# Sorting the values of other items as a row pair, with the first tail laid out by hand

## The chip, the cores and the metric

The kernel runs on one core of a Trainium2 chip. The metric is device time in microseconds (us), measured over whole executions. A trace of one execution gives the span from the first to the last instruction; it is about 2 us shorter than the measured time. The kernel before has a median of 172.65 us. Times in the trace are counted from the start of the span.

## The reference

For each of four items (batch elements) and eight heads, the reference makes a doubly normalised 8 x 8 matrix P from `sort_net`, mixes the eight blocks of 96 keys and of 96 values with it ("sorts" them), attends within each block, and passes the result through a layer with a maximum of two products.

```python
for _ in range(5):                       # P: 4 x 8 x 8 x 8
    P = exp(P - max(P)); P = P / sum(P, -1); P = P / sum(P, -2)
k_sorted = einsum('bhij,bhjcd->bhicd', P, k_blocks)
v_sorted = einsum('bhij,bhjcd->bhicd', P, v_blocks)
attn = softmax(scale * q_blocks @ k_sorted.T)     # within each block
x = (attn @ v_sorted) laid out as 3072 tokens x 512
out = maximum(x @ w1, x @ w2) @ w_out
```

In the text, items are counted from one (item two is `b == 1` in the code).

## The kernel before

TensorE (PE) does nearly everything; VectorE (DVE) and ScalarE (ACT) copy TensorE's results out of its accumulation memory PSUM ("evict" it), exponentiate and normalise; GpSimd (POOL) issues the loads that convert to bf16; SyncE (SP) issues outputs and DMA transposes. The work of one item's feed-forward part is cut into units, and the attention of the next item is strewn between them. What comes after a unit is listed in `tail`, or spread evenly as `steps`.

An item's values fill 64 partitions: two items lie side by side in the 128 rows of `v_raw`. VectorE turns them into `v_dc`, from which TensorE takes its weights. Items one and two are sorted singly (`sort_v`, one row half); items three and four as a pair (`sort_v_pair`, matmuls alternating between the halves).

```python
def load_v(b, c0=0, pieces=2):
    r0 = (b % 2) * 64
    ...
        nc.gpsimd.dma_start(out=v_raw[r0 : r0 + 64, ...], in_=v_src[b, :, ...])

def sort_v(b, t, n=0, eng=None):           # 16 matmuls of one row half, one eviction
    r0, m0 = (b % 2) * 64, (b % 2) * 64
    for m in range(16):
        nc.tensor.matmul(ps[:, m * 64 : (m + 1) * 64],
            v_weights(slice(r0, r0 + 64), t * 16 + m), bd_v[b][r0 : r0 + 64, :], ...)
    evac(...)

def sort_v_pair(b, t, eng=None):           # 8 matmuls of each half in turn, one eviction
    for m in range(8):
        for par in range(2):
            rows = slice(par * 64, par * 64 + 64)
            nc.tensor.matmul(ps[:, par * 512 + m * 64 : ...], v_weights(rows, t * 8 + m),
                bd_v[b][rows, :], ...)
    evac(...)

def x_transposes(b, t, eng=None):          # activations into the layout of the products
    if b:                                  # items two to four: by DMA, issued on SP
        nc.sync.dma_start_transpose(out=xT[:, b % 2, ih, hh]..., in_=x...)
        return
    ...                                    # item one: on TensorE

tail = {
    2: [VA[6], TR[2], VA[7]],
    3: [TR[3], lambda: w2_transposes(1, "A")(), load_rest],       # load_q(1), load_k(2)
    4: [lambda: turn(second, 0)],  ...
    9: [lambda: load_v(2), lambda: load_v(3), lambda: load_k(3)],
    14: [lambda: load_q(2)],
    18: [lambda: pair_q(2, 0), lambda: pair_q(2, 1), lambda: load_q(3)],
}
```

`q_raw` has one buffer, so `load_q(3)` (item four's queries) starts when `pair_q(2)` has read item three's. `xT` is what the products `h` of the next item read; TensorE cannot start them before the transposes have landed.

The softmax here doesn't subtract the row's maximum and nothing guards it: scores larger than these inputs give would overflow.

## Time and profile before

| | before |
|---|---|
| median time | 172.65 us |
| span of the profiled run | 170.8 us |
| TensorE busy | 162.3 us, 95% |
| VectorE, ScalarE busy | 44%, 50% |
| granted TensorE clock (share of full speed) | 0.997 |

This is the answer for four stretches of the kernel before: first tail (up to item two's first product), item two's products up to item three's, item three's up to item four's, and the rest. The columns are the stretch, its length, TensorE's busy time (instructions), the granted clock, the DMA's share and GB/s.

```profile
40.63:74.47 33.84, 32.00 (x436) 1.00 0.94 180
74.47:109.24 34.77, 34.54 (x485) 1.00 0.60 111
109.24:141.25 32.01, 31.77 (x359) 1.00 0.43 100
141.25:167.40 26.15, 26.03 (x147) 1.00 0.23 78
```

### The profile page before, as it was taken

The numbers are of one execution on the slowest core, as the hardware profiler recorded it, in microseconds if no ns is written. First come the engines' busy times: TensorE is split into PE (matmuls) and PEld (weight loads), VectorE is DVE, ScalarE is ACT, GpSimd is POOL, SyncE is SP. The second block draws the span as 40 slices with busy tenths as digits, with TensorE's granted clock in tenths as the row PEclk, the third lists the DMA queues.
The fourth block names the chain that finished last, engine by engine and source line by source line (L and its number), as shares of the span: only waits on it lengthen the run. The fifth ranks groups of instructions, "written<-read, shape, count | busy, mean of one in ns | idle before, by whom it ended". The sixth has DMA issues, their size and how long they took to land.

```text
span 170.8 us, 4526 instructions
## 1 busy us (share of the span) xinstructions
PE 162.3 (95%) x2000; PEld 97.5 (57%) x2019; DVE 75.6 (44%) x174; ACT 85.9 (50%) x104; POOL 29.4 (17%) x44
## 2 busy tenths in 40 slices
PE   7999989999979999999999999999999999999992
PEld 7949655664746454566665455566555455654451
DVE  5978765948525277527742632305432250000011
ACT  4587667684743542446685325265625316652020
POOL 7865585234202000300000000000000000000000
PEclk9999999999999999999999999999999999999998
DMA  3999999999999956699900253592044255000333
GB/s 46 207 205 197 200 207 207 211 204 207 221 213 202 207 120 156 137 168 179 216 19 4 46 169 127 74 273 56 0 35 138 46 175 169 0 0 0 123 139 110
DMA packets 30243, 23.11 MB, mean 135 GB/s; under 512 B 16720, under 2 KB 25168, under 8 KB 30224
## 3 DMA queue, kind: packets, MB, share of 16 engines
q0 software_dynamic: 10880, 12.59, 44.1%
q1 hardware_dynamic: 19200, 10.17, 25.1%
q8 instruction: 16, 0.26, 0.6%
q10 hardware_dynamic: 144, 0.07, 0.1%
q14 instruction: 3, 0.02, 0.0%
HBM read 25.17 MB, written 6.29 MB: 184 GB/s over the span
## 4 chain that ended last, share of the span: by engine, by line
PE 88%; DVE 6%; issue 2%; ACT 2%
PE out_ps L617 35%; PE h_ps L590 23%; PE fill_ps L82 6%; PE wc_ps L570 4%; PE o_ps L488 4%; PE k_ps L394 4%; PE s_ps L461 4%; PE v_ps L415 2%; PE v_ps L436 1%; PE tq_ps L369 1%; ACT e L469 1%; DVE x L505 1%; PE tw_ps L551 1%; DVE qT L110 1%; DVE w2T L110 1%
## 5 line engine op out<-in xcount | busy, mean ns | idle before, releaser
L617 PE MATMUL out_ps<-wo_sb,g 128*128 128x512 bf16 (+2 forms) x188 | 47.0, 371 | 1.1 <-issue 0.3
L590 PE MATMUL h_ps<-xT,w_sb 128*128 128x384 bf16 x256 | 44.8, 327 | 0.4 <-ACT xT L108 0.3
L590 PEld LDWEIGHTS <-w_sb 128*128 128x128 bf16 x256 | 23.9, 97 | 16.2 <-issue 0.7
L108 ACT COPY o<-out_ps 128x1024 f32<-128x1024 f32 x11 | 11.1, 1012 | 40.4 <-issue 22.9
L604 ACT ACTIVATE g<-h_ps 128x768 bf16<-128x768 f32 x27 | 21.9, 810 | 14.8 <-PE h_ps L590 14.8
L469 ACT ACTIVATE e<-s_ps 96x768 bf16<-96x768 f32 x32 | 24.3, 804 | 7.7 <-PE s_ps L461 7.6
L617 PEld LDWEIGHTS <-g 128*128 128x128 bf16 x200 | 16.9, 97 | 15.7 <-DVE x L505 0.4
L617 PE MATMUL out_ps<-wc,xT 128*128 128x512 bf16 (+2 forms) x100 | 24.8, 370 | 0.1
L505 DVE TENSOR_TENSOR x<-o_ps,rs 96x512 bf16<-96x512 f32 x32 | 22.0, 687 | 1.1
L499 DVE RECIPROCAL rs<-o_ps 96x8 f32<-96x8 f32 x32 | 6.4, 201 | 32.1 <-PE o_ps L488 32.1
L617 PEld LDWEIGHTS <-xT 128*128 128x128 bf16 x100 | 9.6, 97 | 11.2
L488 PEld LDWEIGHTS <-e 96*128 96x128 bf16 x256 | 11.7, 97 | 7.0 <-ACT e L469 1.2
L488 PE MATMUL o_ps<-v_sb,e 96*128 96x65 bf16 x256 | 13.1, 193 | 0.4 <-ACT e L469 0.3
L652 DVE COPY o<-out_ps 128x512 f32<-128x512 f32 (+1 forms) x2 | 1.2, 624 | 25.0 <-PE out_ps L617 25.0
L110 DVE CAST v_sb<-v_ps 96x1024 bf16<-96x1024 f32 x8 | 9.7, 1217 | 4.5 <-PE v_ps L415 3.6
L110 DVE CAST kT<-k_ps 128x1024 bf16<-128x1024 f32 x5 | 6.0, 1222 | 12.4 <-PE k_ps L394 12.4
L461 PEld LDWEIGHTS <-kT 64*128 64x128 bf16 x256 | 6.3, 94 | 6.6 <-issue 5.9
L136 POOL DMA_DIRECT2D q_raw<-in_q_dram x7 | 6.4, 936 | 20.5 <-DVE rs L499 14.0
L108 ACT CAST v_sb<-v_ps 96x1024 bf16<-96x1024 f32 x8 | 8.0, 1006 | 2.9 <-PE v_ps L415 1.5
L461 PE MATMUL s_ps<-qT,kT 64*128 64x96 bf16 x256 | 9.0, 204 | 0.5 <-DVE qT L110 0.4
L82 PEld LDWEIGHTS <-fill 128*128 128x128 bf16 x99 | 8.4, 120 | 1.8 <-DVE fill L73 1.2
L82 PE MATMUL fill_ps<-fill 128*128 128x138 bf16 x88 | 7.8, 270 | 1.2 <-DVE fill L73 1.2
(77 smaller groups left out, 138.8 us busy)
## 6 DMA issues: line engine op xcount, KB each, us to landing
out_dram<-o SPq DMA_DIRECT2D x11, 512.0 KB, 3.0
k_raw<-in_k_dram POOLq DMA_DIRECT2D x12, 256.0 KB, 12.1
v_raw<-in_v_dram POOLq DMA_DIRECT2D x6, 384.0 KB, 12.6
q_raw<-in_q_dram POOLq DMA_DIRECT2D x3, 768.0 KB, 12.0
w_sb<-in_moe_w_dram POOLq DMA_DIRECT2D x4, 256.0 KB, 10.0
w_sb<-in_moe_w_dram POOLq DMA_DIRECT2D x2, 512.0 KB, 11.2
wo_sb<-in_moe_w_out_dram POOLq DMA_DIRECT2D x2, 512.0 KB, 14.9
v_raw<-in_v_dram POOLq DMA_DIRECT2D x3, 256.0 KB, 4.9
```

The lines of the kernel that those rows point to most:

```text
L82: nc.tensor.matmul(ps[:, 0:w], w0, fill[:, 0:w], start=True, stop=True)
L108: nc.scalar.copy(out=out_ap, in_=in_ap)
L110: nc.vector.tensor_copy(out=out_ap, in_=in_ap)
L394: nc.tensor.matmul(ps[r0 : r0 + 64, m * 64 : (m + 1) * 64], kv[r0 : r0 + 64, t * 16 + m, :], bd_k[b][r0 : r0 + 64, :], start=True, stop=True,)
L461: nc.tensor.matmul(ps[:, h2 * 512 + ii * 128 : h2 * 512 + ii * 128 + BLK], kT[b][rows, (hp * 8 + i) * BLK : (hp * 8 + i) * BLK + 128], rhs ...
L469: nc.scalar.activation(out=e[:, 0 : 8 * BLK].rearrange("p (t c r) -> p t c r", t=8, r=R), in_=ps[0:BLK] .rearrange("p (t f) -> p t f", t=8 ...
L488: nc.tensor.matmul(ps[:, h2 * 512 + ii * 65 : h2 * 512 + (ii + 1) * 65], e[:, (h2 * 4 + ii) * BLK : (h2 * 4 + ii) * BLK + 128], v_sb[:, m0 ...
L505: nc.vector.tensor_tensor(out=x, in0=ov[:, :, :, 0:D], in1=rs.to_broadcast([BLK, 2, 4, D]), op=ALU.mult,)
L570: nc.tensor.matmul(ps[:, 0:512], w2T[:, fb, dmt * 128 : (dmt + 1) * 128], wo_sb[:, fb, :], start=(fb == 0), stop=(fb == NFB - 1),)
L590: nc.tensor.matmul(h_ps[t][:, m * 512 : m * 512 + TCH], w1_sb[:, hp, fb * 128 : (fb + 1) * 128], xT[:, b % 2, ch, hp % 2, hp // 2, :], sta ...
L604: nc.scalar.activation(out=g, in_=src, func=AF.Relu)
L617: nc.tensor.matmul(dst, g_tiles[b, ch, m // 2][:, m % 2, off : off + 128] if m < NFB else xT[:, b % 2, ch, hp % 2, hp // 2, off : off + 12 ...
```

## The change

The intent: matmuls in two row halves run beside each other, those in one half do not (in the trace 32 sorts take 0.57 us in two halves, 1.04 in one). Before, items one and two were sorted in single halves. The change sorts items three and two as the pair, already in the first tail, and loads item four's values into both halves so that its matmuls can alternate too. The first tail, where all this must fit between item one's last units, is written out by hand.

```diff
-    def load_v(b, c0=0, pieces=2):
-        r0 = (b % 2) * 64
+    def load_v(b, c0=0, pieces=2, half=None):
+        r0 = (b % 2 if half is None else half) * 64
...
     def selections(b):
+        heads = {0: (0, 1), 2: (2, 1), 3: (3, 3)}.get(b)
+        if heads:
+            sel_v[b] = const.tile([G, 2, 8, NB], BF16, ...)
+            for half, item in enumerate(heads):
+                nc.vector.tensor_copy(out=sel_v[b][:, half], in_=ident[..item..]...)
...
+    def sort_v_halved(b, t, eng=None):
+        m0 = (b % 2) * 64
+        for m in range(8):
+            for par in range(2):
+                rows = slice(par * 64, par * 64 + 64)
+                nc.tensor.matmul(..., v_weights(rows, par * 32 + t * 8 + m), bd_v[b][rows, :], ...)
+        evac(...)
...
     def load_rest():
         load_q(1)
+        load_v(2)
         load_k(2)
 
     tail = {
...
+        7: [lambda t=t: sort_k(1, t) for t in range(3)],
+        9: [lambda: q_transposes(1, 0)],
+        10: [lambda: q_transposes(1, 1), lambda: load_q(2), lambda: load_k(3), lambda: turn(both, 0)],
+        11: [SC1[0], SC1[1], lambda: turn(both, 24)],
...
+        14: [lambda: sort_v_pair(2, 0), lambda: sort_v_pair(2, 1)]
+        + [lambda half=half: load_v(3, half=half) for half in range(2)],
...                                        # pair sorts after units 15, 16, 17
+        18: [VA1[0], lambda: pair_q(2, 0), lambda: pair_q(2, 1), lambda: load_q(3)],
+        19: [SC1[4], SC1[5], VA1[1]],
+        20: [VA1[2], TR1[0], VA1[3], TR1[1]],
...
+        23: [VA1[6], VA1[7], TR1[3]],
     }
...                                        # item three: attention follows its keys at once;
...                                        # item four: keys, two visits of sort_v_halved, attention
```

More of the change, by code (lines that the diff above doesn't have):

```diff
@@ L253 @@
     id64 = const.tile([128, 64], FP32, tag="id64", name="id64")
-    maskJ = const.tile([128, 6, NB], FP32, tag="maskJ", name="maskJ")
+    maskJ = const.tile([128, 7, NB], FP32, tag="maskJ", name="maskJ")
     maskM = const.tile([128, 2, 8], FP32, tag="maskM", name="maskM")
@@ L281, in selections @@
     def selections(b):
-        src = ident[0:G, b * 8 : b * 8 + 8]
-        if b % 2 == 0:
-            sel_v[b] = const.tile([G, 16, NB], BF16, tag=f"sel_v{b}", name="sel_v")
-            nc.vector.tensor_copy(
-                out=sel_v[b], in_=ident[0:G, b * 8 : b * 8 + 16].to_broadcast([G, 16, NB])
-            )
+        heads = {0: (0, 1), 2: (2, 1), 3: (3, 3)}.get(b)
+        if heads:
+            sel_v[b] = const.tile([G, 2, 8, NB], BF16, tag=f"sel_v{b}", name="sel_v")
+            for half, item in enumerate(heads):
+                nc.vector.tensor_copy(
+                    out=sel_v[b][:, half],
+                    in_=ident[0:G, item * 8 : item * 8 + 8].to_broadcast([G, 8, NB]),
+                )
         sel_k[b] = const.tile([G, 8, 16], BF16, tag=f"sel_k{b}", name="sel_k")
-        nc.vector.tensor_copy(out=sel_k[b], in_=src.to_broadcast([G, 8, 16]))
+        nc.vector.tensor_copy(
+            out=sel_k[b], in_=ident[0:G, b * 8 : b * 8 + 8].to_broadcast([G, 8, 16])
+        )
     bd_v, bd_k = {}, {}
@@ L300, in block_diagonals @@
                 if m
-                else sel_v[b].rearrange("g h j -> g (h j)")
+                else sel_v[b].rearrange("g two h j -> g (two h j)")
             )
@@ L329, in block_diagonals @@
             else:
-                bd_v[b] = bd_v[b + 1] = bd.rearrange("p m i -> p (m i)")
+                bd_v[b] = bd.rearrange("p m i -> p (m i)")
     v_sb = big.tile([BLK, 128, D + 16], BF16, tag="v_sb", name="v_sb")
@@ L424, in sort_v @@
             ps[0:BLK].rearrange("p (d m) -> p m d", m=64),
+            1024,
+            eng=eng,
+        )
+    def sort_v_halved(b, t, eng=None):
+        m0 = (b % 2) * 64
+        ps = ps_f32("v_ps")
+        for m in range(8):
+            for par in range(2):
+                rows = slice(par * 64, par * 64 + 64)
+                nc.tensor.matmul(
+                    ps[:, par * 512 + m * 64 : par * 512 + (m + 1) * 64],
+                    v_weights(rows, par * 32 + t * 8 + m),
+                    bd_v[b][rows, :],
+                    start=True,
+                    stop=True,
+                )
+        evac(
+            v_sb[:, m0 : m0 + 64, 0:D].rearrange("p m (par d) -> p par m d", par=2)[
+                :, :, :, t * 8 : (t + 1) * 8
+            ],
+            ps[0:BLK].rearrange("p (par d m) -> p par m d", par=2, m=64),
             1024,
@@ L715 @@
         selections(b)
-    for c, n, m in [(2, 1, 0), (3, 3, 1)]:
+    for c, n, m in [(2, 2, 0), (4, 3, 1)]:
         nc.vector.tensor_copy(
@@ L727, in load_rest @@
         load_q(1)
+        load_v(2)
         load_k(2)
+    SC1, VA1, TR1 = att(1)
     tail = {
@@ L732 @@
         3: [TR[3], lambda: w2_transposes(1, "A")(), load_rest],
-        4: [lambda: turn(second, 0)],
-        5: [lambda: turn(second, 24)],
-        6: [lambda: turn(second, 48)],
-        7: [lambda: turn(second, 72), lambda: block_diagonals([(0, 2), (1, 1), (1, 2), (1, 3)], 2)],
-        9: [lambda: load_v(2), lambda: load_v(3), lambda: load_k(3)],
-        14: [lambda: load_q(2)],
-        18: [lambda: pair_q(2, 0), lambda: pair_q(2, 1), lambda: load_q(3)],
+        5: [lambda: block_diagonals([(0, 2), (0, 3), (1, 1), (1, 2), (1, 3)], 2)],
+        7: [lambda t=t: sort_k(1, t) for t in range(3)],
+        9: [lambda: q_transposes(1, 0)],
+        10: [lambda: q_transposes(1, 1), lambda: load_q(2), lambda: load_k(3), lambda: turn(both, 0)],
+        11: [SC1[0], SC1[1], lambda: turn(both, 24)],
+        12: [SC1[2], SC1[3], lambda: turn(both, 48)],
+        13: [lambda: turn(both, 72)],
+        14: [lambda: sort_v_pair(2, 0), lambda: sort_v_pair(2, 1)]
+        + [lambda half=half: load_v(3, half=half) for half in range(2)],
+        15: [lambda: sort_v_pair(2, 2), lambda: sort_v_pair(2, 3)],
+        16: [lambda: sort_v_pair(2, 4), lambda: sort_v_pair(2, 5)],
+        17: [lambda: sort_v_pair(2, 6), lambda: sort_v_pair(2, 7)],
+        18: [VA1[0], lambda: pair_q(2, 0), lambda: pair_q(2, 1), lambda: load_q(3)],
+        19: [SC1[4], SC1[5], VA1[1]],
+        20: [VA1[2], TR1[0], VA1[3], TR1[1]],
+        21: [SC1[6], SC1[7], VA1[4]],
+        22: [VA1[5], TR1[2]],
+        23: [VA1[6], VA1[7], TR1[3]],
     }
@@ L769, in group @@
                 return [lambda: [f() for f in fs]]
-            if b == 0:
-                lo = 8
-                vs = [lambda t=t: sort_v(1, t) for t in range(4)]
-                for m, c in enumerate((0, 24, 48, 72)):
-                    VA[m + 1 : m + 2] = group(VA[m + 1], lambda c=c: turn(both, c))
-                steps = group(*ks) + group(*vs[0:2]) + group(vs[2], qs[0]) + group(vs[3], qs[1])
-            elif b == 1:
-                vs = [lambda t=t: sort_v_pair(2, t) for t in range(8)]
+            attend = group(*SC[0:2]) + VA[0:1] + group(*SC[2:4]) + VA[1:2] + group(VA[2], TR[0])
+            attend += group(*SC[4:6]) + VA[3:4] + group(VA[4], TR[1]) + group(*SC[6:8]) + VA[5:6]
+            attend += group(VA[6], TR[2]) + group(VA[7], TR[3])
+            if b == 1:
                 tail[0] = qs
+                tail[8] = [lambda: turn(both, 0), lambda: turn(both, 24)]
+                tail[9] = [lambda: turn(both, 48), lambda: turn(both, 72)]
                 tail[10] = [lambda: pair_q(3, 0), lambda: pair_q(3, 1)]
-                steps = group(*ks) + group(*vs[0:2]) + group(*vs[2:4]) + group(*vs[4:6])
-                steps += group(*vs[6:8])
-            else:
+                lo = 3
+                steps = group(*ks) + attend
+            elif b == 2:
                 tail[0] = qs
-                lo = 4
-                steps = group(*ks)
-            steps += group(*SC[0:2]) + VA[0:1] + group(*SC[2:4]) + VA[1:2] + group(VA[2], TR[0])
-            steps += group(*SC[4:6]) + VA[3:4] + group(VA[4], TR[1]) + group(*SC[6:8]) + VA[5:6]
-            steps += group(VA[6], TR[2]) + group(VA[7], TR[3])
+                lo = 2
+                vs = [lambda t=t: sort_v_halved(3, t) for t in range(4)]
+                steps = group(*ks) + group(*vs[0:2]) + group(*vs[2:4]) + attend
         done = 0
```

## The prediction

> **What bounds the kernel now.** I read the page first (busy shares, slices, chain), then TensorE's timeline between 40 and 110 us, the waits, and last the DMA landings. The busy row and the chain:
>
> ```profile
> PE 162.3 (95%) x2000; PEld 97.5 (57%) x2019; DVE 75.6 (44%) x174; ACT 85.9 (50%) x104; POOL 29.4 (17%) x44
> ...
> PE 88%; DVE 6%; issue 2%; ACT 2%
> ```
>
> TensorE is busy 95% of 170.8 us and is 88% of the chain that ended last; VectorE and ScalarE are half idle. So a change can win only by taking matmul time away or by closing TensorE's gaps. The waits name the owners of those gaps: about 3 us lie after the last matmul, 1.2 at the start, about 1.2 between 17 and 24 us where the change does nothing. In the stretch that the change lays out anew (40.40 to 74.47 us) TensorE is busy 32.23 of 34.07 us. Its timeline there, with start, length, work and, in brackets, the idle time before it:
>
> ```profile
> 44.09 1.11 PE L415 MATMUL v_ps<-bd,v_dc 64*128 64x64 bf16 x32
> 45.13 1.90 PE L570 MATMUL wc_ps<-wo_sb,w2T 128*128 128x512 bf16 x7
> 46.97 0.38 PE L415 MATMUL v_ps<-bd,v_dc 64*128 64x64 bf16 x7
> 48.34 0.43 PE L415 MATMUL v_ps<-bd,v_dc 64*128 64x64 bf16 x9 [1.00 <-issue]
> ...
> 68.55 1.47 PE L617 MATMUL out_ps<-wo_sb,g 128*128 128x512 bf16 x5 [0.26 <-DVE x L505]
> ...
> 78.91 0.64 PE L436 MATMUL v_ps<-bd,v_dc 64*128 64x64 bf16 x32
> 79.48 1.48 PE L590 MATMUL h_ps<-xT,w_sb 128*128 128x384 bf16 x8
> ```
>
> The reader is to see two things. First, 32 value sorts of item two (one row half) take 45.13 - 44.09 = 1.04 us, 32 of the pair (both row halves in turn) 79.48 - 78.91 = 0.57 us. Second, the only gap of size is the 1.00 us inside item two's third group; the profile sees no releaser for it.
>
> After 74.47 nearly nothing is idle: 34.54 of 34.77 us busy up to 109.24, 31.77 of 32.01 up to 141.25, 26.03 of 26.15 up to 167.40.
>
> **What the Trainium skill says.** "TensorEngine Tiling (Array Packing)", Tiling Modes, Key Properties: tiles of different rows work in parallel, and a change of tiling mode drains the engine. The first agrees: 0.57 against 1.04 us. Of the second the trace shows no separate row; whole groups differ only by about 0.1 us from multiples of their matmuls. "DMA: Bandwidth & Descriptors", Rules for kernel authors: two transfers to the two partition halves serialize. So item four's second copy costs in full; by landings each half of an item's values takes 1.8 us of the stream. The same page, Queues, rings and completion order, says that an engine takes turns between rows at packet granularity. The trace agrees only in part. GpSimd's load of item four's queries began at 67.94 and landed at 79.93; the activation transpose issued on SP at 71.25 landed only at 80.31, 9.1 us later, against a median of 3.0:
>
> ```profile
> DMA to landing us min/median/max: 2.7/3.0/9.1
> ...
> 72.00:76.00 4.00, 4.00 (x36) 2.03 (x35) 1.62 (x4) 1.04 (x2) 0.00 (x0) 1.00 1.12 152
> 76.00:80.00 4.00, 4.00 (x140) 3.01 (x138) 2.14 (x3) 3.22 (x4) 0.00 (x0) 1.00 1.43 128
> ```
>
> (The first line is of the tile xT, the others are stretches; the last two columns are the DMA's share and GB/s.) A transpose behind a large load is late by about 6 us. That cost nothing before: it was needed only by the second half of item two's products at 83.64.
>
> **The change, part by part.**
> 1. Sorts of values. Item two's 64 single-half matmuls go. The pair's 128 now sort items three and two, and item four's 64 alternate between the halves. Instructions stay at 256 matmuls; those in single halves fall from 128 to 64. Gain: 64 x (1.04 - 0.57)/32 us = 0.94 us on TensorE, all on the path. Sixteen evictions remain sixteen, of 1.0 us on ScalarE or 1.2 on VectorE.
> 2. Turning. Before, four half-row copies (3.06 us together) and four of 128 rows (0.82 each); after, eight of 128 rows. VectorE gains or loses 0.3 us, beside TensorE: nothing. The two extra selection copies and the fifth mask product are 0.2 us each at most, nothing.
> 3. The first tail. Four groups of the pair's sort (4 x 0.57 = 2.3 us) move from item two's products into the output products of item one; item two's four (2.2 us with the stall taken out) leave. Keys are sorted about 1.7 us earlier, as the first weight product now follows them. Queries are transposed after the second and third weight products. I lay the groups in the new order, from 40.7 us: key sorts 1.63, four weight products 6.92, two query transposes 1.60, hence first scores at 50.9; then six output pairs at 6 x 2.59 = 15.5, scores 4 x 0.45, values 8 x 0.25, pair sorts 2.3, and about 0.4 for switches. Item two's products start at 72.9 instead of 74.47. The 1.00 us gap and three of 0.16, 0.16 and 0.26 us are then gone: 1.6 us.
> 4. Items three and four. 2.3 us of sorts leave the stretch up to item three's products, 2 x 0.57 = 1.1 us come into the stretch after it.
> Sum without a new wait: -0.94 - 1.6 = about -2.5, so 172.65 - 2.5 = 170.1 us.
>
> **Is the data there?** Query landing at 44.06 leaves 1.5 us before its transposes at about 45.5 to 46. Item three's values take the next 2 x 1.83 us, to 47.7; VectorE's turns, by my layout from 47.3 to 50.6, need the second piece only from the third, at 48.9. Pair sorts stand at 55.5, and their last eviction ends at about 63.0, just when the first value product wants it. These margins are small, but each is positive.
>
> **Rivals.**
> A. The DMA becomes the wait. GpSimd's stream ran without a break to 62.74. Two more value pieces add 3.7 us, so item four's values land at about 66.4 (67.7 with an output between). Item four's queries are issued at about 65.5, and item two's first two transposes at 66.6 and 68.9, straight behind them; before, these were issued at 62.92 and 66.00, ahead of the query load, and landed at 66.52 and 68.77. Products start at 72.9. At the usual 3 us they land at 71.9, in time by 1 us; if they suffer as the later pair did, they land at 75 to 78, and TensorE waits 2 to 5 us. For it: the 9.1 us landing. Against it: the skill's taking turns, and that the load may slip behind. It would make 172 to 175 us.
> B. The 1.00 us gap is not of the order of work but comes again elsewhere, since "issue" has no releaser. Then 171.1.
> C. The last eviction before item two's values, or query transposes of item three (issued at 77.14, landed at 84.88, while scores now want them at about 81), hold TensorE. A stall of 1 to 3 us; not to be added to A in full, since A delays the scores too. Makes 171 to 173.
> D. The dead work leaves but VectorE becomes bound in the laid-out stretch: eight values at 0.85 plus 1.0 of query pairing in the last 9.4 us is 83%. That leaves waits of tenths: 170.5.
>
> **Range and chances.** No wait gives 170.1; A in the middle of its range gives 173.5. I give A (or C of like size) a little over one half, since both the later load and the earlier need point the same way. The mean is near 172.0. Going under 169.2 needs 3.4 us of gain, more than all that I can find: 4%. Over 176.1 needs a wait of 6 us: 7%. Eight in ten: 169.9 to 175.0.
>
> **What would show it.** Right: 256 sort matmuls with 0.57 us per 32 of the pair; no 1.00 us gap at 47; item two's first product at about 73; stretch of item two about 2.3 us shorter, of item three 1.1 longer. Rival A shows as idle time before that first product whose releaser is an xT transpose, with landings above 5 us. I am wrong in the main if TensorE's gaps in the first tail stay as large under other names, or if the time falls below 169.5: then switches of tiling mode or other costs that I left out were worth more than I read.

## The result, and the profile after

The changed kernel takes 177.34 us (median of 4; 176.59 to 177.74), the kernel before 172.93 in the same rounds. The ratio is 1.0251, with a 95% interval from 1.0207 to 1.0296: slower. Ratios are the mean time of one kernel's fast runs over that of the other's in the same rounds, so not quite the ratio of the medians. The prediction's mean, near 172.0, and its range up to 175.0 were both missed.

The busy row and the chain of the page of the changed kernel:

```profile
PE 163.0 (93%) x2001; PEld 96.9 (55%) x2020; DVE 79.3 (45%) x182; ACT 83.4 (48%) x101; POOL 29.4 (17%) x46
...
PE 79%; DVE 8%; DMA 7%; ACT 3%; issue 1%
```

TensorE's share of the chain fell from 88% to 79%, and DMA has 7%: 6% are a transpose into `xT`, absent from the chain before. The same four stretches, in the changed kernel (the second starts at 74.53, where item two's first product could have followed the values at once, as it does in the first experiment):

```profile
41.18:74.53 33.35, 32.62 (x499) 1.00 1.04 199
74.53:112.03 37.50, 33.12 (x361) 0.95 0.54 106
112.03:145.30 33.27, 33.05 (x422) 1.00 0.44 97
145.30:171.50 26.20, 25.97 (x147) 1.00 0.23 78
```

The first stretch is 0.49 us shorter, but starts 0.55 later. The second was to lose 2.3 us of sorts and is 2.73 us longer. The third gains 1.26, as its new sorts say. So the loss lies in the second: 4.4 us there are not busy, and its clock is 0.95. TensorE's timeline, the waits, and the chain at that place:

```profile
74.03 0.65 PE L515 MATMUL o_ps<-v_sb,e 96*128 96x65 bf16 x16
78.66 6.70 PE L617 MATMUL h_ps<-xT,w_sb 128*128 128x384 bf16 x32 [3.99 <-DMA xT<-x]
```

```profile
PE h_ps L617 <- DMA xT<-x: 4.0, 1, 4.0
```

```profile
68.00 10.53 DMA xT<-x
78.53 0.14 issue
78.66 6.70 PE h_ps L617 x32
```

Item two's last values are done at 74.7, its first product starts at 78.66. The transpose that it needs was issued at 68.00 and took 10.53 us. Then the products themselves are slow: 32 of them fill 85.29 - 78.66 = 6.63 us. The granted clock tells why (same columns as above):

```profile
76.00:78.00 2.00, 0.00 (x0) 1.00 1.35 155
...
79.00:80.00 1.00, 1.00 (x5) 0.50 1.14 404
80.00:81.00 1.00, 1.00 (x5) 0.50 1.13 324
```

After the wait TensorE runs at half clock, until about 81.4. At full clock the same 32 products take 5.51 us (in the first experiment), so this costs another 1.1 us. In the trace's record of the clock the half rate lasts 3.41 us, from 78.01 to 81.42.

What stood beside the transposes is told by the trace's record of issue and landing, in us:

```
                     item four's queries   item two's 1st transpose   2nd transpose
before  (issue, landed)   67.94  79.93          62.92  66.52           66.00  68.77
changed (issue, landed)   67.11  78.40          68.00  78.53           70.84  79.14
```

In the kernel before the transposes went first. In the changed kernel the query load was issued 0.9 us ahead of them, and they landed together with it.

### The profile page after: what moved, and what is told of

Read it like the earlier page. It is cut to its first block, busy times and chain, and to the rows that moved or that the text cites. A ratio compares the mean times of both kernels' runs of the same rounds, so it can differ in the third digit from the quotient of the medians.

```text
span 174.8 us, 4537 instructions
## 1 busy us (share of the span) xinstructions
PE 163.0 (93%) x2001; PEld 96.9 (55%) x2020; DVE 79.3 (45%) x182; ACT 83.4 (48%) x101; POOL 29.4 (17%) x46
## 4 chain that ended last, share of the span: by engine, by line
PE 79%; DVE 8%; DMA 7%; ACT 3%; issue 1%
PE out_ps L644 33%; PE h_ps L617 23%; DMA xT<-x 6%; PE wc_ps L597 4%; PE k_ps L398 4%; PE s_ps L488 3%; PE o_ps L515 3%; PE fill_ps L82 1%; PE tq_ps L373 1%; ACT e L496 1%; PE v_ps L463 1%; PE tw_ps L578 1%; DVE qT L110 1%; DMA p_sb<-in_sort_net_dram 1%; PE v_ps L419 1%
## 5 line engine op out<-in xcount | busy, mean ns | idle before, releaser
L617 PE MATMUL h_ps<-xT,w_sb 128*128 128x384 bf16 x256 | 46.3, 333 | 4.3 <-DMA xT<-x 4.0
L631 ACT ACTIVATE g<-h_ps 128x768 bf16<-128x768 f32 x26 | 21.1, 811 | 22.5 <-PE h_ps L617 22.5
L108 ACT COPY o<-out_ps 128x1024 f32<-128x1024 f32 x10 | 10.1, 1012 | 30.1 <-PE out_ps L644 16.9
L515 PEld LDWEIGHTS <-e 96*128 96x128 bf16 x256 | 11.2, 97 | 6.4 <-ACT e L496 1.2
L110 DVE CAST kT<-k_ps 128x1024 bf16<-128x1024 f32 x6 | 7.2, 1222 | 16.0 <-PE k_ps L398 16.0
L633 DVE TENSOR_SCALAR g<-h_ps 128x768 bf16<-128x768 f32 x6 | 5.7, 957 | 8.0 <-PE h_ps L617 7.0
```

The source lines that it names most:

```text
L108: nc.scalar.copy(out=out_ap, in_=in_ap)
L110: nc.vector.tensor_copy(out=out_ap, in_=in_ap)
L515: nc.tensor.matmul(ps[:, h2 * 512 + ii * 65 : h2 * 512 + (ii + 1) * 65], e[:, (h2 * 4 + ii) * BLK : (h2 * 4 + ii) * BLK + 128], v_sb[:, m0 ...
L617: nc.tensor.matmul(h_ps[t][:, m * 512 : m * 512 + TCH], w1_sb[:, hp, fb * 128 : (fb + 1) * 128], xT[:, b % 2, ch, hp % 2, hp // 2, :], sta ...
L631: nc.scalar.activation(out=g, in_=src, func=AF.Relu)
```

## The experiments

Three theories. Theory 1: the transposes stand beside loads issued just ahead of them. Theory 2: the activations, and with them the issues of the transposes, are too late by themselves. Theory 3: it is the bytes of item four's second copy. Twelve kernels were run; all results were correct.

### Holding the query load back

```diff
-        18: [VA1[0], lambda: pair_q(2, 0), lambda: pair_q(2, 1), lambda: load_q(3)],
+        18: [VA1[0], lambda: pair_q(2, 0), lambda: pair_q(2, 1)],
...
+    def load_q3_late():      # after item three's query transposes were issued
+        nc.gpsimd.tensor_copy(out=gate, in_=qT[2][:, 3, R - 1, 0:2])
+        load_q(3)
```

GpSimd's copy waits until item three's query transposes have landed, and the load is behind it. (The text says item two's; the code reads `qT[2]`, item three's.) TensorE's order is the same instruction by instruction.

> The changed kernel, but the load of item four's queries is held back until item two's query transposes have landed (a tiny GpSimd copy that reads them stands in front of it). TensorE's order is unchanged. Theory 1 (the activation transposes of item two stand behind that load in the DMA engines): the 3.99 us wait before item two's first product goes to under 0.5 us, the transposes land in 3 to 4 us instead of 8 to 10, the half-clock stretch goes, and the time falls by about 5 us, from 177.3 to about 171.8. Theory 2 (the transposes are late because the activations and SP's issues are late, 68.0 and 70.8): the wait stays at 2 us or more, time 174 to 177. Theory 3 (the second copy of item four's values, landing until 71.3, is what they stand behind): the wait shrinks by 1 us at most.

Measured: 171.56 us, ratio to before 0.9918 (0.9878 to 0.9958). In TensorE's timeline the products follow the values at once and run at full clock:

```profile
74.31 0.65 PE L515 MATMUL o_ps<-v_sb,e 96*128 96x65 bf16 x16
74.80 5.58 PE L617 MATMUL h_ps<-xT,w_sb 128*128 128x384 bf16 x32
80.31 1.70 PE L398 MATMUL k_ps<-bd,k_raw 64*64 64x64 bf16 x96
```

The first transpose was issued at 68.28, later than in the changed kernel, and landed at 74.03 instead of 78.53. The query load went out at 85.43 and landed at 92.64. So Theory 2 falls: the issues are early enough. All 5.8 us of the loss against this kernel hang on when one load is issued. The slack is small: 74.03 is only 0.77 us before the product starts.

### Item four's values loaded once

```diff
-        + [lambda half=half: load_v(3, half=half) for half in range(2)],
+        + [lambda: load_v(3)],
-                vs = [lambda t=t: sort_v_halved(3, t) for t in range(4)]
+                vs = [lambda t=t: sort_v(3, t) for t in range(4)]
```

> The changed kernel with item four's values loaded once, into the second row half, and sorted from that half alone as before (64 more single-half matmuls). Its query load stays early. Theory 1: 3.7 us less in the load stream, but the query load is still issued at about 67 just ahead of the transposes, so they still wait for it: landing at about 75 to 76, wait 1 to 2 us instead of 4, no or less half clock; sorting costs 0.94 us more; time about 174.5. Theory 3 (the second copy is the cause): wait gone, time about 172.8. Theory 2: wait unchanged, time 178.

Measured: 179.23 us, ratio 1.0357 (1.0312 to 1.0403), slower still. This missed what all three theories expected; Theory 2's 178 is nearest. The first product waited longer:

```profile
79.27 7.57 PE L617 MATMUL h_ps<-xT,w_sb 128*128 128x384 bf16 x32 [4.63 <-DMA xT<-x]
```

The values were all in by 66.93 instead of 71.27, but the query load, issued at 67.09, still landed at 78.93 and the first transpose at 79.14. So Theory 3 falls too: with the load at this place, taking away the copy in front of it does not help. Of the 1.9 us by which this kernel is slower than the changed one, 0.9 are the sorts and 0.6 the longer wait; its half clock lasted 6.83 us instead of 3.41.

### Keeping TensorE busy through the wait

```diff
-        units = [lambda t=t: moe_h(b, 0, t, None if b else "A") for t in range(4)]
+        units = [lambda t=t: moe_h(b, 0, t, None if b else "A",
+                                   n=8704 if b == 1 and t == 0 else 0) for t in range(4)]
```

> The changed kernel with 17 dummy matmuls of 512 columns (about 3.7 us) put into the wait before item two's first product, to keep TensorE busy. If the half clock after the wait (granted clock 0.50 from 78 to 81.4 us) is caused by TensorE being idle, it goes, and 32 products take 5.3 instead of 6.7 us: time about 175.9. If the clock fell for another reason (load, DMA), the time stays at 177.3 or rises.

Measured: 176.25 us (175.28 to 177.13), ratio 1.0193 (1.0137 to 1.0250), 1.1 us less than the changed kernel had in other rounds. The two intervals overlap, so the times alone do not settle the gain. The 17 dummy matmuls ran and the clock stayed up, at 0.996 or more in all four executions, against 0.980 to 0.987 in the changed kernel's:

```profile
74.92 3.83 PE L82 MATMUL h_ps<-fill 128*128 128x512 bf16 x17
79.72 5.61 PE L617 MATMUL h_ps<-xT,w_sb 128*128 128x384 bf16 x32 [0.97 <-DMA xT<-x]
```

The 32 products took 5.54 us (to 85.26) instead of 6.63. So the half clock is a consequence of the idle time, a second price of the same wait. The wait itself stayed: 4.8 us from 74.92 to 79.72, most of it now filled.

### The two first transposes on TensorE

```diff
-        if b:
+        if b > 1 or (b == 1 and t > 1):
             nc.sync.dma_start_transpose(out=xT...)
```

The second of them was also placed two units later, so that TensorE need not wait for its activations.

> The changed kernel with the first two activation transposes of item two done on TensorE (16 matmuls and two evictions of 0.8 us) instead of by DMA. Loads unchanged. Theory 1: the first half of item two's products no longer depends on any transfer, so the 3.99 us wait goes; TensorE has 0.9 us more work; the other two transposes land behind the query load at about 78 to 79, the second half of the products starts at about 82: in time. Item three's query transposes, needed from about 82, land at about 83 to 84: a new wait of 1 to 2 us. Time about 173 to 174.

Measured: 172.10 us, ratio 0.9949 (0.9902 to 0.9997). The wait is gone without touching any load. Item three's first scores waited 0.22 us for their query transposes, less than the 1 to 2 us feared, so the time is below the 173 to 174 expected. By the medians this costs about 0.5 us more than holding the load back, where 0.9 us of extra work was expected; the intervals overlap.

### The query load issued earlier

Pairing item three's queries after unit 16 instead of 18 frees the buffer earlier.

```diff
-        16: [lambda: sort_v_pair(2, 4), lambda: sort_v_pair(2, 5)],
+        16: [lambda: sort_v_pair(2, 4), lambda: sort_v_pair(2, 5)]
+        + [lambda: pair_q(2, 0), lambda: pair_q(2, 1), lambda: load_q(3)],
```

> The changed kernel, but item three's queries are paired on VectorE two units earlier, which frees their buffer earlier, so item four's query load is issued at about 62 instead of 67. The second copy of the values stays. Theory 1, sharpened by the last runs (a transpose lands no earlier than the GpSimd loads that were issued before it): the query load follows the values, which land at about 71, and lands at about 75 to 76; the first two transposes land with it, just after; the wait before item two's first product is 0.5 to 2 us instead of 3.99, without half clock; time about 173. Rival (the query load is slow only because it runs beside the transposes, whenever issued): it lands 10 to 11 us after its start again, at 78 or later; time as the changed kernel, 176 to 178.

Measured: 176.78 us (174.82 to 177.77), ratio 1.0165 (1.0119 to 1.0210). The execution of 177.77 us is over 1.5% above the fastest; the ratio leaves it out, and the median of the other three is 176.13. The load, issued at 63.42, landed at 77.61, the first transpose at 77.80; the wait was 3.44 us, and half clock followed. The 173 us expected were missed, and the rival's 176 to 178 came true, though the load landed at 77.61 and not at 78 or later. By the packet records, 290 of the load's 1024 packets were done by 71, behind the values; after that it shared with the output and the transposes.

> The run before with item four's values loaded once and sorted from one row half (0.94 us more on TensorE). Theory 1: now the 3.7 us of the second copy come off in front of the query load, which lands at about 71; the transposes, issued at about 68 and 71, land by 73 to 74; no wait; time about 172.5, against 173 of the run before although it sorts longer. If the copy has no part in it: the same wait as the run before plus 0.94 us, about 174.

This is the same edit together with the single copy. Measured: 176.22 us (174.37 to 176.70), ratio 1.0188 (1.0143 to 1.0234). Both forecasts (172.5, and 174) were missed. The load landed at 74.92 (not 71), the first transpose at 76.28, and the wait was 1.69 us instead of 3.44. So the copy does count once the load is queued early behind it: 2.7 us earlier landing. The time hardly shows it, because this variant sorts 0.94 us longer and lost more to half clock: the 32 products took 7.24 us (76.42 to 83.66) instead of 5.51. In this run the profile puts the wait down to VectorE, but the activation had been done long before the transpose's issue at 68.05; what came at 76.28 is the transpose.

### What the sorts are worth

> The kernel with the held-back query load, with item four's values loaded once and sorted from one row half. No wait in either; so the difference to the kernel with the held-back load (171.56) is the worth of sorting from both halves: 64 matmuls x 14.7 ns = 0.94 us, plus at most 0.3 for one or two more visits. Expected 172.5. If sorting from both halves is worth nothing on the path: 171.6.

The held-back load together with the single copy, 5 rounds: 172.06 us, ratio 0.9973 (0.9952 to 0.9994), against 0.9918 with both copies. The difference of 0.0055 is 0.95 us. Sorting groups as they stand in the trace, from each group's start to the next group's, take 4.60 us from 23 us on, against 3.68 in the next run, which sorts from both halves: 0.92 us. This agrees with the 0.94 us of the prediction. The run shows one thing more: without the second copy, and with the query load held back, the first transpose landed at 71.29 instead of 74.03. So the copy's bytes do delay the transposes, by 2.7 us; in the held-back kernel the slack hides it.

### The selection copies behind the normalisations

```diff
-    for b in range(1, B):
-        selections(b)
-    ...                                   # and the mask copies
     def load_rest():
         ...
+        for b in range(1, B):
+            selections(b)
+        ...
```

> The kernel with the held-back query load, with the selection and mask copies on VectorE moved behind the last two normalisations of item one. In the changed kernel six extra small copies stand in front of them and item one's last transpose waits 0.51 us instead of 0.23. Expected: that wait goes to under 0.2, the rest moves up, time 0.3 us less than 171.56, about 171.2. If something else holds the stretch: no change.

Measured, 5 rounds: 170.83 us, ratio 0.9895 (0.9874 to 0.9917). Item one's last transpose, first in the held-back kernel, then here:

```profile
34.56 0.52 PE L553 MATMUL tx_ps<-ident,x 96*128 96x96 bf16 x8 [0.52 <-DVE x L532]
```

```profile
33.59 0.51 PE L553 MATMUL tx_ps<-ident,x 96*128 96x96 bf16 x8
```

The wait is gone. By ratio the gain is 0.0023, or 0.4 us. In the traces item two's first product starts 0.8 us earlier (74.00 against 74.80), of which 0.52 are this wait. The intervals of the two overlap, so the size of the gain is not settled.

### A dummy load with long rows

In the held-back kernel, the same 768 KB were loaded at the old place, but with rows of 6 KB.

```diff
+    def load_decoy():                      # called where load_q(3) was
+        t = qpool.tile([128, H, R * D], BF16, tag="q_raw", ...)
+        src = v[3].rearrange("h (p c) d -> (h p) (c d)", p=16)
+        for m in range(2):
+            nc.gpsimd.dma_start(out=t[m * 64 : m * 64 + 64]..., in_=src[m * 64 : m * 64 + 64])
```

> The kernel with the held-back query load, plus a dummy load of the same bytes (768 KB) at the place and time where the changed kernel issues item four's queries (about 67), but with rows of 6 KB instead of 768 bytes; what it brings is overwritten later. Theory 1a (any GpSimd load issued just ahead holds the transposes): they land about when the dummy load does, at 76 or later, TensorE waits 1.5 us or more, time 174 to 177. Theory 1b (it is the short rows of the query load, which run badly beside transposes): the dummy load is done by about 74 and the transposes land by 75; wait under 0.7 us; time about 172.

Measured: 176.78 us, ratio 1.0247 (1.0201 to 1.0292); wait 3.63 us. The load's second half landed at 75.78, the first transpose at 77.85. So it is not the short rows of the queries: a load of this size with long rows, at this place, does it too. How the two queues share is seen in the trace's DMA packet records. I counted the packets of GpSimd's queue and of SP's that ended in a stretch (what a count leaves over are 4-byte packets and, in the third row, 11 packets of the output, in the fifth 18):

```
run, stretch (us)       GpSimd's queue          SP's queue
changed, 64 to 68       144 (112 of 6144 B)     144 (144 of 2048 B, output)
dummy load, 70 to 73    100 (82 of 6144 B)      105 (103 of 2048 B, output)
changed, 72 to 75       567 (567 of 768 B)      434 (421 of 256 B, transposes)
changed, 73 to 75       349 (349 of 768 B)      336 (336 of 256 B, transposes)
held back, 72 to 75       0                    1208 (1124 of 256 B, transposes)
values once, 72 to 75   536 (536 of 768 B)      135 (135 of 256 B, transposes)
```

In the first two rows and the fourth the queues finish nearly equal numbers of packets: they take turns packet by packet. (In the third, the transposes began only at about 72.) A turn is worth the size of a packet: in the first row the output moved 295 KB while the loads moved 688, and in the fourth the transposes, with 256 bytes, moved a third of what the queries moved. Alone they finished 1124 packets in the time in which they finished 421 beside the load. And SP's queue is one line: the output issued at 67.29 in the changed kernel, in front of the transposes, landed at 73.27, the one before it, issued at 59.73, only at 71.46. With the dummy load the output in front, issued at 66.96, landed only at 76.48. So part of the transposes' delay is time spent behind outputs that a load held up; no run moved the outputs away, so this part was not measured by itself. In the last row the transposes had even less than their turn; why, I leave open.

### The extra copy in the old order

```diff
-        9: [lambda: load_v(2), lambda: load_v(3), lambda: load_k(3)],
+        9: [lambda: load_v(2), lambda: load_v(3), lambda: load_k(3), load_again],   # to a spare tile
```

> The kernel before with item four's values loaded once more into a spare tile, behind its key load and before item three's queries, as the changed kernel does. If what costs is the order of query load and transposes and not the bytes: the first two transposes, issued at 62.9 and 66.0, land a few us later (about 69 to 72) but are wanted only at 74.5; time within 0.5 us of the kernel before. If the extra 3.7 us of loading cost by themselves: 2 us or more slower.

Measured: 173.14 us, ratio 1.0028 (0.9990 to 1.0067). The first two transposes landed at 68.06 and 68.85, far ahead of 74.5. In the old order, with its slack, the extra bytes cost nothing clear of noise. (In the changed kernel the copy stands behind item three's queries, not in front of them as the text says.) This run also shows again the 1 us gap within item two's third sort:

```profile
48.37 0.43 PE L415 MATMUL v_ps<-bd,v_dc 64*128 64x64 bf16 x9 [1.11 <-issue]
```

It belongs to that order of instructions; in no run of the new order does it come back. Its cause was not tried. One candidate: in both traces a 16 KB packet of the queue that the profile calls "instruction" runs just before the gap (from 45.95 us for 0.89, and from 46.05 for 0.95), while in the changed kernel it comes at 44.83, during the long weight products. TensorE may thus have waited for its own instructions; this is not shown.

### Pairing the queries later

The kernel with the later selections, with item three's pairing moved behind item two's last values:

> The kernel with the held-back load and the later selection copies, with item three's query pairing also moved behind the last values of item two, which takes 1.0 us of VectorE from in front of the activations. TensorE's order is unchanged. Expected: item two's transposes issued about 1 us earlier; no wait before its products as before; item three's query transposes, ready later, are still in time; time 170.8 or up to 0.3 less. If the later pairing makes item three's scores wait: up to 1 us more.

Measured, 5 rounds: 170.93 us, ratio 0.9898 (0.9866 to 0.9931). No gain over 0.9895. The 0.30 us wait in the laid-out tail, for ScalarE's copy of an output, is still there, and the first transpose was issued at 67.66 against 67.49, not 1 us earlier. A miss without consequence.

### Half the load

Only four of eight heads of the query load at the old place, the others held back:

```diff
+        18: [VA1[0], lambda: pair_q(2, 0), lambda: pair_q(2, 1), lambda: load_q_half(0)],
...                                        # load_q_half(1) behind the gate, as in the first run
```

> The changed kernel, with only half of item four's queries (four heads, 512 packets of 768 bytes instead of 1024) loaded at the early place; the other half is held back behind item two's query transposes. Turn-taking by packets (equal numbers of packets of both queues finish while both have work, so the transposes' 1536 packets of 256 bytes gain on the load only after it ends): half as many foreign packets, so the transposes land about half as much later than in the held-back kernel (74.0): about 76; wait 1 to 2.5 us instead of 3.99; a half-clock stretch may still follow; time 173.5 to 176. Rival, all or nothing (any load ahead costs the full wait): wait about 4 us, time 177.

Measured: 173.47 us (173.37 to 174.89), ratio 1.0067 (1.0003 to 1.0131). The half landed at 75.40, the first transpose at 76.40:

```profile
76.54 5.64 PE L617 MATMUL h_ps<-xT,w_sb 128*128 128x384 bf16 x32 [1.70 <-DMA xT<-x]
```

The dose works: first transpose at 74.03, 76.40 and 78.53, and waits of under 0.15, 1.70 and 3.99 us, for no load, half and the whole. No half clock followed in the profiled execution, although 1.69 us of waiting in the earlier run did bring it. The clocks of the two runs at the same place, first of this run, then of the early load with a single copy:

```profile
78.00:80.00 2.00, 2.00 (x14) 1.00 2.01 249
```

```profile
78.00:80.00 2.00, 2.00 (x8) 0.50 1.77 218
```

"TensorE: Matmul & The Clock Gate", Part 1, says that the default state is half rate, that activity releases it, and that the window in which it is judged runs free of the kernel. The filled wait and these two runs agree with that: idle time brings the half clock, and a wait of 1.7 us brings it in some executions only. By the mean clocks it is not a matter of the kernel: in the run of this section one execution of four has 0.990 (and 174.89 us), the others 0.996 or more; in the earlier run three have 0.988 or 0.989 and one 0.998 (and 174.37 us). The page's rule to avoid gaps of over about 3.4 us is too mild here, as the run at 0.50 shows.

## Why the prediction was wrong

- **What bounds the kernel.** Right. TensorE's gaps decided it, and the other engines' added work mattered only where TensorE waited for it.
- **Sorts of values, 0.94 us.** Right: 0.95 by times, 0.92 in the trace.
- **Turning and selections, "nothing".** Wrong by a little. The selection copies stand in front of item one's last normalisations; the transpose behind waited 0.51 instead of 0.23 us, and moving them was worth about 0.4 by ratio.
- **The first tail, 1.6 us.** Too high; this term failed. The 1.00 us gap did go. But the two gaps of 0.16 us were never there: where the trace of before has them, one matmul record is missing (5 instead of 6 in one group, 1 instead of 2 in the other), and the groups take as long as elsewhere (1.75 us from 57.92 to 59.67, and again from 96.64 to 98.39). And my layout had item two's products ready to start at 72.9, while TensorE was free for them at 74.53. Of the 1.6 us between, 0.5 was there when the keys were sorted (41.18 against 40.7). 0.3 are the four weight products, put at 6.92 us, which take 7.21; one alone took 1.83 in the kernel before. 0.5 belong to a new wait for an output's eviction (0.30 us idle before 67.31; the rest is the end of the group before it, which otherwise overlaps with the next). 0.4 are the switches: the six output pairs took 16.35 us, 0.8 more than 15.5, and I had allowed "about 0.4"; six output matmuls take 1.39 us in front of a pair sort or of scores, against 1.30 in front of values. Without any wait for transfers the kernel takes 171.56, not 170.1; the term "-2.5" measured -1.4 by ratio.
- **Items three and four.** Right: the third stretch grew by 1.26 us for 1.1 of sorts, and in the held-back kernel, where no wait hides it, the second shrank from 34.77 to 32.25 us (74.80 to 107.05) for 2.3.
- **"Is the data there?"** Right for queries, values and turns: none of the margins was passed, though the last pair eviction ended at 64.44, not 63.0, just ahead of the value product at 64.50. The transposes were not in this list but in Rival A.
- **Rival A.** Its mechanism came true: the query load issued at 67.11 (I had 65.5), the transposes at 68.00 and 70.84 behind it, and landings at 78.53 and 79.14, just beyond the 75 to 78 given. That the wait of 3.99 us lies within its 2 to 5 is partly luck: the landing was later than I said, and so was the moment at which TensorE was free (74.53 instead of 72.9). Item four's values, too, landed at 71.27 and not at 66.4 to 67.7, as the last three pieces took 2.3 us each beside an output, not 1.83.
- **The step that failed.** It is the landing of the first transpose, which I left open between "the usual 3 us" (71.9, in time) and 75 to 78. I gave this rival "a little over one half", and took the mean. It was no matter of chance: issued behind the load, the transpose took 10.53 us, and wherever item two's products needed the transposes with the load in front TensorE waited (1.69 to 4.63 us, and 4.8 with the wait mostly filled); without the load it never did. The evidence was in hand: a transpose behind the same load had taken 9.1 us. I set against it "the skill's taking turns". But turns by packets speak for the wait, not against it, as the packets of a transpose have 256 bytes and those of the load 768. "Over 176.1 needs a wait of 6 us" failed with it: 4 us were enough, because the kernel without a wait takes 171.56, not 170.1, and because the wait brought the half clock.
- **The half clock** was in no rival, though a wait of this length was in my list. It cost 1.1 us in the trace: 6.63 against 5.51 us for 32 products (5.54 with the wait filled).
- **The terms together.** 170.1 + 1.1 (gain over-read, 2.5 against 1.4) + 0.3 (the kernel before took 172.98 in those rounds, not 172.65) = 171.5, the kernel without the wait. From there to 177.34 are 5.8 us. The two traces account for 4.9 of them, mainly the wait (4.1 from 74.53 to 78.66) and the half clock (1.1), less 0.3 by which the changed kernel's trace was ahead before it. The profiled execution is the fastest of the four, with the least half clock (0.987 against 0.980 to 0.981 in the others), which fits the rest.
- **Rivals B and D.** B: the gap did not come again in the new order. D: VectorE held up nothing beyond the 0.51 us. **Rival C** is seen only as 0.22 us, in the run with transposes on TensorE.

The version that beats both is the changed kernel with the query load held back and the selection copies moved: 170.83 us, ratio 0.9895 (0.9874 to 0.9917). The idea of the change was good for about 1%. A load in the wrong place cost three times that.

## What to carry to other kernels

When work moves so that a transfer's result is needed sooner, look at what is issued just ahead of that transfer, on any queue, and not only at its usual landing time. Here the queues took turns by packets (349 and 336 in 2 us), so a transpose in packets of 256 bytes fell behind a bulk load until that load was nearly done: in every run with such a load in front, the first transpose landed between 0.03 us before the load and 2.1 us after it. Hold the bulk load behind a dependency when nobody needs it soon. If a mechanism has been seen once in the trace of before and the change brings the same order about at a place with no slack, give it its full weight, and add the slow clock that a TensorE wait can bring with it.

## What the Trainium skill lacked or had wrong

- "DMA: Bandwidth & Descriptors", Queues, rings and completion order: the turns by packets are confirmed (144 and 144, 349 and 336 of what the trace calls packets; whether these are the page's packets, which it puts at several descriptors, is not shown), but it does not say what follows: the share goes by packet size, so the DMA transposes (256 bytes) finished 421 packets in 3 us beside a load of 768-byte packets and 1124 alone, and a landing rose from a median of 3.0 to 10.5 us. In one run (values once, 135 against 536 packets) it had less than its turn; neither page nor runs explain that.
- The same page, Rules for kernel authors: "A transpose next to ordinary DMAs needs nothing" holds for correctness; in time it cost up to 4.63 us of TensorE here.
- The same rules, two transfers to the two partition halves: by landings each of item four's four pieces took 1.7 to 2.3 us in the changed kernel, so the second copy did not come free, and it delayed the transposes behind it by 2.7 us; but in the old order it cost nothing clear of noise (ratio 1.0028, 0.9990 to 1.0067).
- "TensorE: Matmul & The Clock Gate", Part 1: the rule there names gaps of over about 3.4 us; a wait of 1.69 us was followed by a clock of 0.50 in one run, a wait of 1.70 us by none in another.
- "TensorEngine Tiling (Array Packing)", Key Properties, says that a change of tiling mode drains the engine, without a cost; here six output matmuls took 1.39 us in front of matmuls over 64 rows (pair sorts, scores), against 1.30 in front of matmuls over 96 rows (values).
